# 28 filler matmuls ahead of the first TensorE operation of a fused attention and MLP kernel

## The chip, the cores and the metric

The kernel runs on one core of one Trainium2 chip. The metric is the time of one execution on the device in microseconds (us), lower is better; the median of three runs is compared.

## The reference

Four batches with eight heads, 768 positions and 64 dimensions per head. Each query may look only at six chunks of 32 keys, chosen by an upper bound; the result goes through a two-layer network with an ELU between.

```python
k_min, k_max = k_chunks.min(3), k_chunks.max(3)          # chunks of 32 keys
ub = sum(maximum(q * k_min, q * k_max), -1)              # bound per query and chunk
ub = where(causal, ub, -1e9)
top_chunks = argsort(ub)[..., -6:]
scores = where(in top_chunks and causal, (q @ k.T) / sqrt(64), -1e9)
attn_out = softmax(scores) @ v                           # (4, 8, 768, 64)
x = attn_out.transpose(0, 2, 1, 3).reshape(3072, 512)
h = x @ w_in                                             # 512 x 2048
g = where(h > 0, h, exp(minimum(h, 0)) - 1)
out = g @ w_out                                          # 2048 x 512
```

## The kernel before

The kernel first builds a list of operations (`g.op(...)`), each with its name, the engines that may run it, and the tiles that it reads and writes. Nothing is scheduled by a planner when it runs: the string `ORDER` writes the order out by hand. Each entry has three characters: the engine (P is TensorE, A ScalarE, D VectorE, G GpSimd, S the DMA queue of SyncE) and the serial number of the operation in two digits of base 64. Operations are emitted in that order, so each engine works through its own entries strictly in sequence. The string `PLACES` gives, for every tile that appears for the first time in that order, the slot of its class that it takes. The class `bank` stands for the eight PSUM banks.

```python
for j in range(0, len(order), 3):
    o = g.ops[64 * DIGITS.index(order[j + 1]) + DIGITS.index(order[j + 2])]
    for b in o.bufs:
        if b.slot is None and b.cls != "fixed":
            b.slot = DIGITS.index(next(places))
    o.emit({"P": PE, "A": ACT, "D": DVE, "G": POOL, "S": SP}[order[j]])
```

The work is cut in eight units of 384 token rows. Units 0 and 1 hold the first halves of batches 0 and 1. For them the keys and queries are loaded in pieces of 96 rows and turned by TensorE through `ident_f` (operations `kT...` and `qT...`, line 402, four f32 transposes each). VectorE reduces the keys to chunk bounds (`kmin...`, `kmax...`, line 367), and ScalarE or VectorE copy the results out of PSUM (`kt...`, `qh...`, line 320 or 322). Before the scores of the first six chunks, where no selection is needed, a mask is put into the bank by a matmul with `trineg` (`tr...`, line 676), then come the scores (`sc...`, line 684, eight matmuls), the exponentials (`ex...`, line 692) and the products with the values (`pv...`, line 746). Behind each unit's attention stand the two layers of the network: `h<unit>.<block>` (line 843, four matmuls for each of 16 column blocks of `w_in`), the exponential `e` (line 850), `m` (line 852), `g` (line 856) and the output product `o` (line 867). The network of one unit is woven between the attention of the next ones.

`w_in` is loaded by GpSimd's queue in three pieces (line 291: column blocks 0 to 3, 4 to 7, 8 to 15), `w_out` in four (line 297). Loads of `q`, `k` and `v` go into eleven slots `f` and are issued by SyncE (line 304), the first ones for `k` by ScalarE.

A filler is an operation `fill` (line 906): one matmul of a 128x128 tile of zeros with a 128x256 tile of zeros, both bf16, into a bank that nobody reads. 170 of them stand in the list of operations, and `ORDER` of the kernel before uses three, between the first transposes and masks. The tile `zeros` is set by VectorE (operation `zeros`, entry `D00`), as its sixth memset. TensorE's first entry in the kernel before is `P0M`, the key transposes `kT0p1` of batch 0.

Of the kernel before, what the change touches and what calls it, by code (L numbers as in the profile page):

```python
# [41 lines left out]
D0OD1iP1yA0LP0TS0ZPjTP1lS2hA0UA1nG16P1oGmvP1qA1sP2oGmwA1mG0-S2OD2pP18D19D13S2PP1tP1uP1vG0pA0AP1N  # L42
P1DD2qP1EA1rP25A1xA2sG0JP26A1wP1zP1AA1CG10P1ID27P1RGmxG0eG0fP1HS2RP1SD1FG0PP20D1GD28D0SGmyD1JD1K
P2aP1XA1BP1+P29G1dD1TP1YD1UP1LA1MP2wA2xP2BA2FG2HD1ZD2bD2cD1-P1OD1PP2dA2eD1QP1VA1WD21D22D12P23P2J
G2uG14A2KD24PmWAmXD2DD0oA2yGmYD2rPmSAmTPn2S2vA2ND2CG2EPm-Am+GmUGn0D2LP3lAn3DmZPmOAmPG2zDmVD3mD3n
D3pGn4Dn5PmKAmLDn1D3oGmQA2APmCAmDGmMS2ID3qGmzP38D39PmGAmHS2QGmIPnyPniDmND3rA3cAnzGnAAnjGmADmRD3a
DnkDmJPneAnfDnBA2tDnlPn6GmEA3sAn7PnaPnmAnbP3HDmFA3IGn8Dn9PnuGncAnvPnqD3tDndP3gAnnGnoGnwD3hA2GA3u
P33G3bA34A35G07P2XD2ZD2YG08A2+DnxA36DnpPnIS2VD3iGngG3jD2-S2mS3fAnrGmBG31G2WP3+A40PnPPnQD30P3JA3K
DnhP3wPnCPnDD2MD3yS2kG3vP4DD3xS32D3zD3AD3BP4jA4kD3CG3EGnsDntPnRD01S50A3FD37S2TS4ZP41A42D43S4-PnE
PnJA3dP4sA3DD2nP3QP3SA4EA4tA3TS4+S4XP4FA3RP4lG3LPnKP4aG3eA4bP48A49D2lG3US4YD2jP3NS55A4GAbeP3MD3O  # L50
G3GPnLP4MP45A4ND3kD3PG2SP4OA4PPnFA4mG4cPnSP4uAnGDnMS53G2UP4dP4eP3VG4QP44P4RAnTS7OP4SA4vD0nG4wSat
D4HP5QA5RA5SP4ID4nP4JD4fD4gD46D47P4oP3WG5TS7NP4hG5UA4iP4pD4TSnND4UP5rD3XD4qP5EA5FA5sG5uG7PD4KD4L
P4yP4xD3YS7LG5IP4VA4WP5JA5ND4zP3ZA3-P5kA5oD4rP58D4AP4BA4CD5KD5aD5LP5fA5gA5jP5xD5yPnZPoBAn-A5tA5i
S7SPopPodAoCD5lG5OD5cD59D5mSauGn+Do0G5eAoqDorA5hDoDG5nSnHG5MS5wAoeGofD5zG5APoxSnUAoyA54G56DoEPot
AouPo1GovDogDosDowAo2Go3A5GPnVAnWDo4GozG5bDoAPoJAoKS57Po9GnXAoaPo5Ao6A5HDoLDoMGobDnYDocA5dG5vA5B
PolGo7Do8AomGonP5VSaFD5XA7TD5WD5YD5ZPohAoiGojS7UPoVG5qPoFAoGA5PDooGbdPp6Po+DokPoWPoXPp7A02D5-D5+
A63A61D60P6lP6gP64ShvP6iG5pP6mA6jPp0P66S7QD7RDoHDoIA65DaGDaHA6hD62DaJA67A6nD6oP6aA6bP6uPp1P6yA6z
PoRP68A6vS51D52P6eA6fPoNA69SazAoSSavD6kP6cP6qAoOP6IPp8A6dP6pDaIDoPA6JGoTP6wA6xDoQG5DP6GDoUS7JPoY
SaKDaLDaNA6HD6KAoZG5CP6YP6MP6LA6NP6-A6ZA6+P70Pp9P6AGbjD6rA71P6EP72A73A6FPp2ScPDaMA6BScKP6CP76A6D
P74DpaP79DaOG6OP6QD6sA75A77D78P6PD6RP7aA7bD7cP7uS7MP7wA7xP7zD6SS7KS7IP7VD7WP6UA7vP6WA6VA6XSo-P7s  # L60
A7tP7ADaPP8uD8vP7mP7dD7XD7yS6TP7qA7BG7CS6tP7eD7fA7rA7nP7iDp3P7oP7kP8cA7jP85DaQA7lD7gS7hP7DA7pP7E
D8dD89G8bA8yP8pD7FD7GA8qDcQS7HA8zSaXP8iGaRPaSDaVDaWD8AP80A81D8jD8aDbkP8BA7ZA8CA8FA8DG7-D8kD8lD8w
# [36 lines left out]
AwzPw2PwiSvBGw8GwcDwdPwCAw3Dw4Dw5GwADwBPwePwIPwJAwnAwfPwuGwgDwhAwjDwkDwlPwqGwoPwOPwUAwvDw9PwKAwr
DwsDwtPwDPwEDwwDwxDwpPwFAwGSwHPwLAwMSwNPwPPwQPwRAwSSwTPwVPwWPwXAwYSwZ  # L100
"""
PLACES = """
0123450678900012310a451621724113347405105762041730373120422137035110122041374503402021750562104
11700021501212164000111000232317000261024540320151612783210206940a4115b7020263230c2d08313907563
e427013111610f2462a4157230523415317204500240181232917400132164442027121011015390433401070102214
32165110232322g012012404027056912362011513002222138302a1074000501632b12e00470a54532710053007754
3536761803040210c4d7000070514641470501540276062053123358047315654477500103751216120371201004305
1133301272500002f20031113622203117a520g015450281601270b0118e52632041024101400915211067296022454
34100764021c31306064002235167402302130631214236547406210120001573201632930716102101011702313220
34020122261030220031d151423237101000022511407221g060001258340e12213140f20009272162ab30510344272  # L110
# [845 lines left out]
```

## Time and profile before

| | |
|---|---|
| median of three runs | 286.16 us (286.0 to 286.5) |
| the profiled execution | 287.72 us, its span 286.0 us |
| TensorE matmuls busy | 267.4 us, 93% of the span |
| VectorE busy | 222.7 us, 78% |
| ScalarE busy | 208.8 us, 73% |
| GpSimd busy | 117.3 us, 41% |
| moved by DMA | 39.25 MB, mean 137 GB/s |

The span goes from the first to the last instruction of the profiled execution. Busy shares are means over stages that have different limits, and a matmul's recorded length overlaps with that of the next one, since matmuls are pipelined; the spacing of their starts is what each one costs in a row of them. PE is TensorE's matmul, PEld its weight load, DVE VectorE, ACT ScalarE, POOL GpSimd, SP SyncE; a q behind the name (SPq, ACTq, POOLq) is the sequencer of that engine, where DMAs are issued.

### The profile page before, as it was taken

To read this page: it belongs to the slowest core of one execution; us is meant where nothing else is said; L and a number is where in the kernel's file an instruction comes from. 1 tells how busy PE (TensorE), PEld (TensorE's weight loads), DVE (VectorE), ACT (ScalarE), POOL (GpSimd) and SP (SyncE) were. 2 spreads that over 40 slices of the span, in tenths; PEclk is the share of its full clock that TensorE was granted. 3 is DMA by queue.
4 is the path that set the end of the run, shared out by engine and by line. 5 is a ranking of instruction groups with operands and counts; after the bars stand their busy time and mean duration, and the time that the engine had idled before them with its cause. 6 is when DMAs were issued, how large, how long until landed. Compare 5 with 4: busy or idle time off the path is not lost.

```text
span 286.0 us, 6892 instructions
## 1 busy us (share of the span) xinstructions
PE 267.4 (93%) x2415; PEld 163.0 (57%) x2415; DVE 222.7 (78%) x674; ACT 208.8 (73%) x463; POOL 117.3 (41%) x244
## 2 busy tenths in 40 slices
PE   0898999999999899999999989899999999999995
PEld 0656665685455655476565545566556556665553
DVE  1649897689988999889799989997796989621760
ACT  0567795899599896998789569696779469792722
POOL 7484775667321275340352313501555043320510
PEclk9999999999999999999999999999999999999999
DMA  8999999979848299657984738345851420013103
GB/s 154 212 196 218 223 220 213 215 153 267 169 112 166 57 201 227 152 116 166 193 178 97 149 87 206 71 124 119 172 125 27 93 87 2 17 39 78 73 2 110
DMA packets 107107, 39.25 MB, mean 137 GB/s; under 512 B 98496, under 2 KB 102848, under 8 KB 107072
## 3 DMA queue, kind: packets, MB, share of 16 engines
q1 hardware_dynamic: 100208, 33.83, 56.6%
q0 software_dynamic: 3696, 4.19, 8.6%
q10 hardware_dynamic: 3168, 0.79, 1.7%
q8 instruction: 19, 0.31, 0.5%
q14 instruction: 16, 0.13, 0.2%
HBM read 30.41 MB, written 6.29 MB: 128 GB/s over the span
## 4 chain that ended last, share of the span: by engine, by line
PE 52%; DVE 20%; ACT 10%; DMA 5%; POOL 4%; issue 4%; SPq 3%; ACTq 0%; POOLq 0%; DVEq 0%
PE bank L867 17%; PE bank L843 14%; PE bank L774 8%; DVE gT L856 5%; PE bank L825 4%; ACT pt L789 4%; DMA xt<-on 3%; DVE kst L367 3%; DVE thr L611 3%; PE bank L543 2%; DVE m L852 2%; DMA f<-in_v_dram 2%; PE bank L592 2%; SPq L304 2%; PE bank L402 2%
## 5 line engine op out<-in xcount | busy, mean ns | idle before, releaser
L843 PE MATMUL bank<-xt,w_in_sb 128*128 128x384 bf16 x512 | 90.8, 326 | 2.2 <-DMA xt<-on 2.0
L867 PE MATMUL bank<-w_out_sb,gT 128*128 128x512 bf16 (+1 forms) x400 | 92.3, 370 | 0.0
L852 POOL TENSOR_SCALAR m<-e 128x384 f32<-128x384 f32 x90 | 46.6, 524 | 69.3 <-ACT e L850 57.8
L856 DVE SCALAR_TENSOR_TENSOR gT<-bank,m 128x384 bf16<-128x384 f32 x128 | 67.0, 549 | 7.9 <-POOL m L852 5.9
L850 ACT ACTIVATE e<-bank 128x384 f32<-128x384 f32 x128 | 59.2, 491 | 17.5 <-PE bank L843 11.5
L789 ACT ACTIVATE pt<-bank 128x384 bf16<-128x384 f32 (+1 forms) x144 | 67.3, 552 | 4.5 <-PE bank L774 4.3
L843 PEld LDWEIGHTS <-w_in_sb 128*128 128x128 bf16 x512 | 49.4, 98 | 37.0 <-issue 5.7
L867 PEld LDWEIGHTS <-gT 128*128 128x128 bf16 x400 | 37.7, 97 | 35.2 <-DVE gT L856 1.0
L774 PE MATMUL bank<-rhs,lhs 96*128 96x384 bf16 (+2 forms) x240 | 44.6, 293 | 2.2 <-DVE gT L856 0.8
L774 PEld LDWEIGHTS <-lhs 96*128 96x128 bf16 x240 | 21.7, 97 | 16.8 <-issue 3.7
L320 ACT ACTIVATE o<-bank 128x512 f32<-128x512 f32 (+1 forms) x17 | 9.8, 576 | 21.6 <-PE bank L867 19.7
L825 PEld LDWEIGHTS <-pt 128*128 128x128 bf16 x576 | 21.0, 97 | 4.9 <-DVE rcp L636 0.6
L806 POOL TENSOR_TENSOR pt<-pt,tri 128x256 bf16<-128x256 bf16 (+1 forms) x12 | 10.7, 895 | 29.4 <-ACT pt L793 16.2
L852 DVE TENSOR_SCALAR m<-e 128x384 f32<-128x384 f32 x38 | 15.4, 409 | 9.0 <-ACT e L850 8.8
L825 PE MATMUL bank<-vext,pt 128*128 128x65 bf16 x576 | 22.2, 193 | 0.1
L367 DVE TENSOR_REDUCE kst<-bank 128x12 f32<-128x384 f32 x32 | 16.6, 547 | 6.3 <-PE bank L402 3.2
L638 DVE TENSOR_TENSOR on<-bank,rcp 128x384 bf16<-128x384 f32 (+1 forms) x40 | 19.7, 502 | 1.1
L322 POOL CAST rhs<-qt 64x384 bf16<-64x384 f32 x23 | 11.5, 501 | 21.0 <-DVE qt L322 13.0
L806 DVE TENSOR_TENSOR pt<-pt,tri 128x512 bf16<-128x512 bf16 (+1 forms) x36 | 13.6, 390 | 4.8 <-ACT pt L793 3.1
L402 PE MATMUL bank<-ident_f,f 96*128 96x96 f32 x64 | 10.1, 318 | 7.5 <-POOL ident_f L254 7.5
L543 PE MATMUL bank<-ident_f,f 128*128 128x128 f32 x96 | 15.0, 277 | 0.8 <-ACT pt L789 0.7
L636 DVE RECIPROCAL rcp<-bank 128x6 f32<-128x6 f32 (+1 forms) x40 | 7.0, 182 | 10.6 <-PE bank L825 4.2
(101 smaller groups left out, 316.8 us busy)
## 6 DMA issues: line engine op xcount, KB each, us to landing
f<-in_v_dram SPq DMA_DIRECT2D x22, 256.0 KB, 4.7
out_dram<-o SPq DMA_DIRECT2D x21, 256.0 KB, 2.4
f<-in_q_dram SPq DMA_DIRECT2D x18, 256.0 KB, 4.6
f<-in_k_dram SPq DMA_DIRECT2D x18, 256.0 KB, 4.6
kc<-in_k_dram SPq DMA_DIRECT2D x8, 384.0 KB, 4.2
w_out_sb<-in_moe_w_out_dram POOLq DMA_DIRECT2D x4, 512.0 KB, 8.3
f<-in_q_dram SPq DMA_DIRECT2D x6, 192.0 KB, 5.0
w_in_sb<-in_moe_w_in_dram POOLq DMA_DIRECT2D x2, 512.0 KB, 7.5
```

Source lines behind the costliest of these rows:

```text
L367: g.op(("kmin", "kmax")[w] + tag, (DVE,), lambda e, w=w, op=op: nc.vector.tensor_reduce(out=cs(w), in_=src(), axis=AX.X, op=op), reads=[(b ...
L543: nc.tensor.transpose(ap(bk)[:, P * j:P * (j + 1)], ap(src[j])[:, P * r:P * (r + 1)], ident_f)
L638: g.op("on" + tag, (DVE,), lambda e: nc.vector.tensor_tensor(out=ap(on)[:, 0:nt].rearrange("p q h d -> p h q d"), in0=view()[:, :, :, 0:D] ...
L774: nc.tensor.matmul(ap(banks[hd])[:, o + pc:o + pc + wd], lhsT=apl(ls, G)[0:96, pr, hd, P * kb:P * (kb + 1)], rhs=ap(rs)[0:96, hd, c0 - HS ...
L789: lambda e, hd=hd, pt=pt, banks=banks, wtot=wtot: nc.scalar.activation(out=ap(pt)[:, hd, PAD:PAD + wtot], in_=ap(banks[hd])[:, 0:wtot], fu ...
L806: eng[e].tensor_tensor(out=view, in0=view, in1=tri[:, 64:64 + P].rearrange("p (a b w) -> p a b w", a=1, b=1) .to_broadcast([P, 2, len(dg), ...
L825: nc.tensor.matmul(view()[:, hd, qi, :], lhsT=ap(pt)[:, hd, P * qi + off:P * qi + off + P], rhs=ap(vx[b])[:, kb, 2 * r + hd, :], start=(kb ...
L843: nc.tensor.matmul(ap(bank)[:, 0:HS], lhsT=w_in_sb[:, kk, P * fc:P * (fc + 1)], rhs=ap(xT[i, kk]), start=(kk == 0), stop=(kk == NKK - 1))
L850: g.op(f"e{i}.{fc}", (ACT,), lambda e, eb=eb, bank=bank: nc.scalar.activation(out=ap(eb), in_=ap(bank)[:, 0:HS], func=AF.Exp), reads=[(ban ...
L852: g.op(f"m{i}.{fc}", (POOL, DVE), lambda e, eb=eb, mb=mb: eng[e].tensor_scalar(out=ap(mb), in0=ap(eb), scalar1=-1.0, scalar2=1.0, op0=AOT. ...
L856: nc.vector.scalar_tensor_tensor(out=ap(gt), in0=ap(bank)[:, 0:HS], scalar=0.0, in1=ap(mb), op0=AOT.max, op1=AOT.min),
L867: nc.tensor.matmul(ap(bank)[:, 0:d1 - d0], lhsT=ap(gts[fc])[:, P * tt:P * (tt + 1)], rhs=w_out_sb[:, fc, d0:d1], start=(fc == 0), stop=(fc ...
```

## The change

Only the two strings change. `ORDER` gets 28 more fillers directly ahead of `P0M`, so that they are the first 28 operations of TensorE; the three fillers further on stay where they are and only take the next serial numbers. `D00`, the memset of `zeros`, moves from its place behind five other VectorE memsets to the head of the list. All other entries keep their order.

`PLACES` gets a bank for each of the 28 fillers, which take the banks 0 to 7 in turn. Every later operation takes bank b + 4 where it had bank b below 4, and b - 4 where it had one of 4 to 7; slots of all other classes are the same.

```diff
 ORDER = """
-D0cG0gG0jD0hG0lG06S0XS0BD09A0uD0kS0xG0dD03A0sG04A0rA0tA0WG0qA0VS0vD00S0YG0bS0zS0wS0yG0aP0MA0QA0R
-D05P1pP1jPjRGcZD0iD0NS2iD0mP0DP1aD0CD0ED0FG0GP11A15G17PjSS2gS2fD1cS0+P1kD1eD1fG1gA0HA0IP1hD1bP0K
...
+D00D0cG0gG0jD0hG0lG06S0XS0BD09A0uD0kS0xG0dD03A0sG04A0rA0tA0WG0qA0VS0vS0YG0bS0zS0wS0yG0aPjRPjSPjT
+PjUPjVPjWPjXPjYPjZPj-Pj+Pk0Pk1Pk2Pk3Pk4Pk5Pk6Pk7Pk8Pk9PkaPkbPkcPkdPkePkfPkgP0MA0QA0RD05P1pP1jPkh
+GcZD0iD0NS2iD0mP0DP1aD0CD0ED0FG0GP11A15G17PkiS2gS2fD1cS0+P1kD1eD1fG1gA0HA0IP1hD1bP0KD0OD1iP1yA0L
...
 PLACES = """
-0123450678900012310a451621724113347405105762041730373120422137035110122041374503402021750562104
...
+01234506789012345670123456701234567012340056710a01122132411734300114536200133437756402253307515
...
 """
```

More of the change, by code (lines that the diff above doesn't have):

```diff
@@ L45 @@
[L45 to L62, printed above, removed]
@@ new lines @@
+P25A1xA2sG0JP26A1wP1zP1AA1CG10P1ID27P1RGmxG0eG0fP1HS2RP1SD1FG0PP20D1GD28D0SGmyD1JD1KP2aP1XA1BP1+
+P29G1dD1TP1YD1UP1LA1MP2wA2xP2BA2FG2HD1ZD2bD2cD1-P1OD1PP2dA2eD1QP1VA1WD21D22D12P23P2JG2uG14A2KD24
+PmWAmXD2DD0oA2yGmYD2rPmSAmTPn2S2vA2ND2CG2EPm-Am+GmUGn0D2LP3lAn3DmZPmOAmPG2zDmVD3mD3nD3pGn4Dn5PmK
+AmLDn1D3oGmQA2APmCAmDGmMS2ID3qGmzP38D39PmGAmHS2QGmIPnyPniDmND3rA3cAnzGnAAnjGmADmRD3aDnkDmJPneAnf
+DnBA2tDnlPn6GmEA3sAn7PnaPnmAnbP3HDmFA3IGn8Dn9PnuGncAnvPnqD3tDndP3gAnnGnoGnwD3hA2GA3uP33G3bA34A35
+G07P2XD2ZD2YG08A2+DnxA36DnpPnIS2VD3iGngG3jD2-S2mS3fAnrGmBG31G2WP3+A40PnPPnQD30P3JA3KDnhP3wPnCPnD
@@ new lines @@
+D2MD3yS2kG3vP4DD3xS32D3zD3AD3BP4jA4kD3CG3EGnsDntPnRD01S50A3FD37S2TS4ZP41A42D43S4-PnEPnJA3dP4sA3D
+D2nP3QP3SA4EA4tA3TS4+S4XP4FA3RP4lG3LPnKP4aG3eA4bP48A49D2lG3US4YD2jP3NS55A4GAbeP3MD3OG3GPnLP4MP45
+A4ND3kD3PG2SP4OA4PPnFA4mG4cPnSP4uAnGDnMS53G2UP4dP4eP3VG4QP44P4RAnTS7OP4SA4vD0nG4wSatD4HP5QA5RA5S
+P4ID4nP4JD4fD4gD46D47P4oP3WG5TS7NP4hG5UA4iP4pD4TSnND4UP5rD3XD4qP5EA5FA5sG5uG7PD4KD4LP4yP4xD3YS7L
+G5IP4VA4WP5JA5ND4zP3ZA3-P5kA5oD4rP58D4AP4BA4CD5KD5aD5LP5fA5gA5jP5xD5yPnZPoBAn-A5tA5iS7SPopPodAoC
+D5lG5OD5cD59D5mSauGn+Do0G5eAoqDorA5hDoDG5nSnHG5MS5wAoeGofD5zG5APoxSnUAoyA54G56DoEPotAouPo1GovDog
@@ new lines @@
+DosDowAo2Go3A5GPnVAnWDo4GozG5bDoAPoJAoKS57Po9GnXAoaPo5Ao6A5HDoLDoMGobDnYDocA5dG5vA5BPolGo7Do8Aom
+GonP5VSaFD5XA7TD5WD5YD5ZPohAoiGojS7UPoVG5qPoFAoGA5PDooGbdPp6Po+DokPoWPoXPp7A02D5-D5+A63A61D60P6l
+P6gP64ShvP6iG5pP6mA6jPp0P66S7QD7RDoHDoIA65DaGDaHA6hD62DaJA67A6nD6oP6aA6bP6uPp1P6yA6zPoRP68A6vS51
+D52P6eA6fPoNA69SazAoSSavD6kP6cP6qAoOP6IPp8A6dP6pDaIDoPA6JGoTP6wA6xDoQG5DP6GDoUS7JPoYSaKDaLDaNA6H
+D6KAoZG5CP6YP6MP6LA6NP6-A6ZA6+P70Pp9P6AGbjD6rA71P6EP72A73A6FPp2ScPDaMA6BScKP6CP76A6DP74DpaP79DaO
+G6OP6QD6sA75A77D78P6PD6RP7aA7bD7cP7uS7MP7wA7xP7zD6SS7KS7IP7VD7WP6UA7vP6WA6VA6XSo-P7sA7tP7ADaPP8u
@@ new lines @@
+D8vP7mP7dD7XD7yS6TP7qA7BG7CS6tP7eD7fA7rA7nP7iDp3P7oP7kP8cA7jP85DaQA7lD7gS7hP7DA7pP7ED8dD89G8bA8y
+P8pD7FD7GA8qDcQS7HA8zSaXP8iGaRPaSDaVDaWD8AP80A81D8jD8aDbkP8BA7ZA8CA8FA8DG7-D8kD8lD8wA82G84A8ED7+
+PpEApFD86D8xPpMApNPpgD87ShuGbgGpGDpHD8rGpODpPA8mPpcApdGpeDpfPpIPpwApJGpKAphA8eD8fApxG7YA8gPpoG88
+DpLPpAApBGpiDpjA8sGpCDpDPpQSaBApRGpyG83DpzP8GD8ID8KAppScMGpSDpTPpsAptGpuSayDpvAaCPpkPq0SnOPq4ScT
+GpqAplScRAq1AcSD8HGpmAq5PpYDpnA8tD8JApZGq6DprGp-PpUS8hAcUScJAaAPq8PqoPqpAq9D8LD8MApVDq7PqcPqdGpW
+DpXA8NP8TP8+Dp+SaDP8VPqqSawAaEScOA90A8WGqaDaYSpbG8OP8RDqbAaTDaUA8UP93A94Dq2A8SP91DaZDq3P96P97A98
@@ new lines @@
+GbhSaxSbiA92ScNDa+P8XA8YPqeP8ZA8-Sb0P9tA9uP9rA9sPqrD8QPafAagD95D99P9aD8PP9pA9qP9fP9bD8oPahD9cD9d
+A9gG9vP9lA9mP9nA9oGcVP9xP9wA9yDqsPqfG8nDqgP9jPalAaiP9hA9iA9kPbrDa-P9LP9TA9UP9RA9SDbsP9XP9WA9YG9z
+P9BP9AP9NA9OA9MShpDb1D9CD9ZD9DS9EPd2PadP9FA9GPakSqhP9PA9QP9JA9KDajPabAacP9HShzGcYD9VDb2PbBA9IPa3
+Aa4Pa5Aa6Db4AaeP9-DbCP9+AamPbmDa0SflDa1Pa7Pa9AaaPqiDanAa8DbuS9ePapDbFGbESa2DbnPaoDaqAboAd3PbwAbx
+DarDb3PqjPqkPqlDb6SasDbyDbvDb5AbqAqmDbtGb7PdhSqtPb8Db9DbbPqyGbAAqzDbcPqOAqPAcWGqQDfmDfnAbaSp4AbD
+DqADqBDqRPraArbPquGrcPqCAqDAbpDrdPbGDbHAdiDbJAqvPdcAd4AddPriPr2GqEArjDqFDqwPd7DbIDbKGrkAr3Gr4Drl
@@ new lines @@
+DbLPqWAqXDbMPr6Ar7Gr8DqxDr9PqGAd8DqYDqZPreAqHPqSScLDc+AbOAqTPrqDbNPqKGbQDr5GqIDqJAbPArrGrsDrtAqL
+SblSbfPc3Ac4ScXGqUPrmDqMDqNDqVSfaArnGbzPq-Aq+Dr0PbTAbUPrADr1PbWArfPbXAhIGrgSc-DfpAbYPc5Ac6Dc7PrB
+PcBPbRAbSDfoPcmSf9SqnDg0PcASfqAd0PcxAcyPrCDdaPruAcCAdePc8PcjPc9PcvDd9PcnGcDGroDrhPrvPrwAckAcwSfj
+Sd1DbVDbZPb+AcaDcbPcdPchDczPcEPb-AcoShtDrpDd5AciDc0SfbPccDc1Sc2DcePcFDcfAdbScgPrDDcGDcpAdjGclGhw
+DcHScIPdmArESrFDdnPcqPcrDcsDctPrGScuPrxAryAf+PrHPrIPrJDdpAdfArKPsgAshDdoDdqDdrDdsPscAsdPrQAduDfr
+DfsPrYArRDdtPdBGdlDseArZDsfDsiDsjAdCGd6PdzDfuPe5PsoAe6Gr-Dr+AspDsqAdAGrSSfcDrTPrMArNPdHAdIPs4As5
@@ new lines @@
+GrODrPPrUDfWArVGrWGhASfIPsAPe9SfeAsBDsrPdFAdGDrXPs8As9AeaDsCPe3Ae4PskSrzDs6PdJDsDPswDs7DdvPsIPe7
+AslDsmPs0DsnAsxPsMDsaPdXGsyDszAsJSfdDsKAdKAs1Gs2DsLPdOAhCDs3PdPAdQGfZPsEAdYPdLPdDAdEAdMShrDsbPsN
+GdgAsFAe8PdxSg1DftAdyDfwSffPdZPssPsSGfkAd-DdNDdRPdTDfvGfxDdwPedAstDsuPfyDfzAfADsvPdSDdUDdVSdWDeb
+Pe1Ae2DfJAfBAfCDfKPsTPd+PecAe0SrLAeePexDefPezGfYPeCPeDAeEAfVPsODeFPenAeADfMPevAewGsGDsHSfDPehAey
+PegAeoDeiDejDeBSekGdkPghGhBPetAeuPsPAsQPeXPelAemPf1DfLPeZPf0DgiPg2PepAf2PsUAeqPerPeGDg3Gg6Dg4AeY
+AesAe-PeNAeOPeLPeVAeMDe+PePPeHPeRDeISp5DeJShsPeTSeKPg7Dg8Gf3AeQPsVDsWSsXAeUAeSPgcPf4AeWPf5DfEDf6
@@ new lines @@
+AgdDf7PsYPsZAglPhKAhLGhOPs-DfFDfHAgkDggPs+Sf8AgeDfODfGDfNGfPPtGPtuDg9AhHPfQAt0AtHGtIDfTAfUDtJPtC
+AtDDtEAfRDfSDtFAtvGtwDtxAgjGgfPtiPtaAtbGtcPgmDgoAhMPt6At7GfgGt8PteAtfGtgDgqDtdDgnDgpShDDgrPtmAtn
+GtoDt9PtKAtLGtMDgsPt2At3PtSAtjAguDtpDtNGtkDtlPtWSsRPtqPtyGt4SfXDgtPt-PtODt5AgvDthPu8AtrDtsDttDg5
+Sf-PgxAtXPgzGtYDtZAtTAtzPu9GtADtBSfhPhUPhPAtPGtUDtVShqAhEAgyPuaAgwPhgDgbDtQAt+DtRPhbAgAGgBSt1AhQ
+AhVAhcGhYAhRPgRPhdDu0AhePgCPgDAgEDgFPu2Pu3DhXGgaPgQAgSDhfPh3DhWPhhAhiGhFPgZShxShGAg-Ph2Ah4GfiPhZ
+Ah-Pg+Ah0Ah+GhyPu4PgNDgTAgOShJDu1PgGPgHDgIDhjPubDh1AucGh5DgJPhlPhkPh6SgKPh7Dh8Dh9ShaPgLAgMDgPDhm
@@ new lines @@
+75005073116165203312010007011533301232104002f20035113262203113a120g015050285201270b4118e1623204
+102010140495121106329242205434104760025c7130602004267552704230617023125067214344665012000113724
+523697475210610145130271322030020122225430620031d111027233501004026111403221g020041258740e52613
+104f20009232122ab301107402324206467152030441173621638553677472060413523016121060250211131117200
+106002c2044526141022757235611d50020141210a30017200b5e4722121612032a2100851f33074166151921437225
+1710121012325314075090502322720315076123242061767030185313012620122100131014523001g722410536201
@@ L118 @@
+01004223100a0701d5220112036c1e047256f0121130422120730701352322283024216407500321422674632794210
+3740356112501226421110761300124220b14305052060a1021d310f41112210113554062272e0144607362025c0711
+0g17240220335617001413080061202730634561711635203445023471212702451302030227010129150004124600a
+16011305230041015612b12322142c01e02311f01708d2012
 """
```

70 lines of the change are left out of this document (15 added, 55 removed).

## The prediction

> **What bounds the kernel now.** I read the page first (span, busy shares, the forty slices), then the chain of waits for the first 30 us, then the timeline of TensorE alone there, and last those of VectorE, ScalarE and GpSimd.
>
> ```profile
> span 286.0 us, 6892 instructions
> ...
> PE   0898999999999899999999989899999999999995
> ...
> PEclk9999999999999999999999999999999999999999
> ```
>
> TensorE is busy in nearly every slice but the first, which is empty: nothing runs there for 7.46 us. The granted clock reads full throughout, so if the array is slow anywhere, that row does not say so; durations must.
>
> ```profile
> 7.46 0.90 PE L402 MATMUL bank<-ident_f,f 96*128 96x96 f32 x4 [7.46 <-POOL ident_f L254]
> 9.68 0.42 PE L906 MATMUL bank<-zeros 128*128 128x256 bf16 x1
> 9.89 2.13 PE L402 MATMUL bank<-ident_f,f 96*128 96x96 f32 x12
> 11.81 0.42 PE L906 MATMUL bank<-zeros 128*128 128x256 bf16 x1
> 12.03 0.63 PE L676 MATMUL bank<-trineg,ident_b 128*128 128x512 bf16 x1
> 12.46 1.58 PE L402 MATMUL bank<-ident_f,f 96*128 96x96 f32 x8
> 15.81 0.61 PE L684 MATMUL bank<-xt,kt 64*128 64x64 bf16 x8
> 21.52 0.40 PE L684 MATMUL bank<-xt,kt 64*128 64x64 bf16 x8
> 25.70 0.83 PE L661 MATMUL bank<-ident_b,on 128*128 128x128 bf16 x8 [0.67 <-ACT xt L320]
> 26.37 0.50 PE L402 MATMUL bank<-ident_f,f 96*128 96x96 f32 x4
> ```
>
> In each row stand the start, the length (both us), the engine, line, operation and tiles, and the idle time before it with what ended it. The same four transposes take 0.90 us at 7.46 and 0.50 at 26.37; the same eight score matmuls 0.61 at 15.81 and 0.40 at 21.52. So the array runs at about half speed from its first instruction to a little after 21 us, and at full speed afterwards, whatever the clock row says. Those are the 14 us that the change can touch. In them TensorE sets the end only for a part:
>
> ```profile
> 7.46 0.92 PE bank L402 x4
> ...
> 8.45 1.28 ACT L320
> ...
> 10.27 0.56 DVE kst L367
> ...
> 13.77 0.48 DVE kst L367
> ...
> 14.29 0.58 PE bank L676
> ...
> 20.36 0.94 PE bank L746 x15
> ...
> 21.96 0.60 ACT pt L692
> ```
>
> The chain goes through TensorE for the first four transposes, through ScalarE and VectorE from 8.45 to 14.25, and through TensorE again from 14.29 to 21.9. Only the first and the last of these gain from a faster array.
>
> **The change part by part.** *The fillers' own cost.* They need only `zeros`, whose memset moves to the head of VectorE's queue.
>
> ```profile
> 0.96 0.38 DVE L247 MEMSET econst<- 32x384 bf16 x1 [0.96 <-PEq L940]
> 2.60 0.17 DVE L247 MEMSET zeros<- 128x128 uint32 x1
> 9.26 0.15 PEld L906 LDWEIGHTS <-zeros 128*128 128x128 bf16 x1 [0.28 <-issue]
> ```
>
> VectorE starts at 0.96; 0.17 us of memset, about 0.05 us of hand-over and 0.15 us of weight load put the first filler at about 1.33. A slow filler is recorded at 0.42 us, but the matmul behind it starts 0.21 (9.68 to 9.89) and 0.22 us (11.81 to 12.03) later: matmuls overlap, and the price is about 0.213. 28 of them take 5.97 us and free the array at 7.30. The first transposes wait for `ident_f` until 7.46, so the fillers lie wholly in an idle stretch, with 0.16 us to spare; once the clock rises they go faster still. At 0.22 each they would end at 7.49 and cost 0.03. If the cover were gone, each filler would cost its 0.21 in full. The five VectorE memsets that `zeros` is moved past start 0.17 us later. `ident_f`'s own memset stands just ahead of the 2.60 of this row, and the first transposes are released by GpSimd's work on it only at 7.46, so that costs nothing. No queue of loads is touched. All later PSUM banks are renumbered by one fixed swap of 0-3 with 4-7, so who waits for whose bank stays the same: nothing.
>
> *What the fillers buy.* The trace shows when the clock rises in the kernel before (just after 21 us, at the end of a dense run of score and value matmuls) but not how much work it takes, so this is bounded from both sides: no release before 7.46 (nothing gained), or a full release (below). I take the release, since almost 6 us of back-to-back 128-row matmuls are denser than the mix of transposes, short matmuls and waits that did not suffice between 7.46 and 21. [...]
>
> With the array fast from 7.46 on:
> First transposes: 0.90 becomes 0.50, so the table load at 8.45, the copy and all of VectorE's run from 10.27 to 14.25 come 0.40 earlier. That run itself is not shortened.
>
> ```profile
> 13.70 1.01 DVE L367 TENSOR_REDUCE kst<-bank 128x12 f32<-128x384 f32 x2
> 15.70 0.49 ACT L320 ACTIVATE xt<-bank 128x384 bf16<-128x384 f32 x1 [1.14 <-PE bank L402]
> 16.46 0.60 ACT L692 ACTIVATE pt<-bank 128x512 bf16<-128x512 f32 x1 [0.27 <-PE bank L684]
> 17.54 1.08 ACT L692 ACTIVATE pt<-bank 128x512 bf16<-128x512 f32 x2 [0.48 <-PE bank L684]
> 20.40 0.60 ACT L692 ACTIVATE pt<-bank 128x512 bf16<-128x512 f32 x1 [0.78 <-PE bank L684]
> 21.27 1.78 ACT L692 ACTIVATE pt<-bank 128x512 bf16<-128x512 f32 x3
> ```
>
> The reduce pair ends at 14.71, or 14.31 after; it frees the bank for `qT0p1`, whose four transposes then take 0.50: done at about 14.85, and ScalarE's copy `qh0p1` starts at 14.9 instead of 15.70. That is 0.8 in all. From there ScalarE becomes the bound: between 15.70 and the exponential at 21.96 it waits for TensorE 0.27 + 0.48 + 0.78 = 1.53 us and works the rest. With scores in half the time these waits go, and nothing shortens the exponentials. So at 22 us the kernel is at most 0.8 + 1.53 = 2.3 us ahead.
>
> *What is late next.* Weights. The first layer's last eight column blocks of `w_in` come in one GpSimd load, here with its issue, its time to landing, and the matmuls that use it:
>
> ```profile
> 19.82 0.79 POOL L291 DMA_DIRECT2D w_in_sb<-in_moe_w_in_dram  x1
> DMA to landing us min/median/max: 12.4/12.4/12.4
> 32.50 4.71 PE L843 MATMUL bank<-xt,w_in_sb 128*128 128x384 bf16 x28
> ```
>
> It lands at 32.2. Of the 28 matmuls the first four (`h0.1`) use the earlier load; the fifth (`h0.15`) starts at 32.50 + 4 x 0.168 = 33.17, less than 1 us after the landing. TensorE 2.3 us ahead would want it at 30.9. How far the load moves I bound by 0.4 (its queue on GpSimd moves with the VectorE run) and 2.3 (it moves with TensorE). I take 0.4, since the transfers around it queue rather than idle: 12.4 us for 1 MB. It then lands at 31.8, and 33.17 - 31.8 = 1.4 us is what remains, because TensorE runs without a gap from there through all 28. Behind it I find no load that comes closer to its user than this, so I carry 1.4 us to the end: the work there waits for work, not for a fixed time.
>
> Sum: span 286.0 - 1.4 = 284.6; the profiled execution's own 287.72 becomes 286.3, and the median of the three runs, 286.16, becomes 284.8. A difference under 0.2% (0.6 us) is about what a measurement of this kernel cannot tell from none.
>
> **The rivals.** *The load is no limit* and the whole 2.3 us survives: 283.9. For it: loads ahead of it are issued earlier as well, so the engines may have time left. Against: it took 12.4 us in a full queue.
>
> *The release fails or is lost again.* [...] The trace speaks against the loss: around 25.70 a stretch of transposes with a wait of 0.67 leaves the clock up. [...] Then at most the first 0.40 us remains: 285.8 to 286.2, no difference.
>
> *The fillers outlast their cover*: slower. If each cost its recorded 0.42 us, because every one waits for the one before or for its weights, 28 take 11.8 us, from 1.33 to 13.1, and the first transposes start 5.6 us late; 2.3 come back through the fast array and some 3.3 remain: 289.5. The turning point is sharp: (7.46 - 1.33) / 28 = 0.219 us each, and up to about 0.30 the gain still pays for it (28 x 0.08 = 2.2). Against it stand the two spacings of 0.21 and 0.22, though each is of one filler among other matmuls and none of fillers in a row on cycling banks.
>
> **How the numbers follow.** Forecast (released, load-limited) 0.50; load no limit 0.18; no release or lost again 0.18; fillers outlast their cover 0.10; the rest, 0.04, for a reshuffle of loads and queues that gives most of the gain back. Predicted 284.8. The range reaches from the full 2.3 us with a little over (283.5) to the no-difference case (286.5, the slowest of the runs shown); it leaves out the slower rival. Faster by over 0.2%: 0.50 + 0.18 and a little of the third, 0.70. Same: 0.18. Slower: 0.12.
>
> **What would show it.** Right: 28 fillers between about 1.3 and 7.3 on TensorE, spaced 0.21 and then 0.11; the first four transposes still at 7.46 but in 0.50 us; eight score matmuls near 15 in 0.40; ScalarE without waits between 15 and 20; the exponential of 21.96 near 19.7; TensorE waiting before `h0.15` for a load. Wrong: transposes still at 0.90; the first of them later than 7.5, released by nothing but TensorE itself; a VectorE run that does not come forward; or a front that is 2 us ahead at 22 us while the end is not.

## The result, and the profile after

| | changed kernel | kernel before, beside it |
|---|---|---|
| median of 11 runs each | 285.39 us (285.04 to 285.93) | 286.68 us (286.0 to 288.84) |
| the profiled execution | 285.42 us, span 283.7 us | 287.72 us, span 286.0 us |

The ratio is 0.9945, with a 95% interval of 0.9924 to 0.9966: the change makes the kernel faster by about 0.55%, or 1.6 us. (The means of the eleven runs, 285.42 and 287.00, lie 1.6 us apart, the medians 1.3. The profiled execution of the kernel before is 1.0 us above its median, so two profiles compared show a larger gain than the runs do.) Forecast were 284.8 us in a range of 283.5 to 286.5, and faster with a chance of 0.70. So the size came out as forecast. The runs below show that the reason did not.

First the page of the changed kernel, with the rows that stood in the prediction for the kernel before, and the row of q8, a queue of instructions that becomes important further on:

```profile
span 283.7 us, 6948 instructions
...
PE   8788999999999899999999999899999999999995
...
PEclk9799999999999999999999999999999999999999
...
q8 instruction: 19, 0.31, 0.5%
```

The empty first slice is filled. The clock row now has a dip in its second slice. The timeline of TensorE (start, length, engine, line, operation and tiles, idle time before with its releaser) shows the first 36 us:

```profile
1.14 6.10 PE L907 MATMUL bank<-zeros 128*128 128x256 bf16 x28 [1.14 <-DVE zeros L248]
7.48 0.55 PE L403 MATMUL bank<-ident_f,f 96*128 96x96 f32 x4 [0.24 <-POOL ident_f L255]
...
10.44 1.54 PE L403 MATMUL bank<-ident_f,f 96*128 96x96 f32 x8 [0.50 <-DMA f<-in_k_dram]
...
15.09 0.40 PE L685 MATMUL bank<-xt,kt 64*128 64x64 bf16 x8
...
25.33 1.96 PE L844 MATMUL bank<-xt,w_in_sb 128*128 128x384 bf16 x11 [0.64 <-DMA w_in_sb<-in_moe_w_in_dram]
...
31.52 0.47 PE L403 MATMUL bank<-ident_f,f 96*128 96x96 f32 x3 [0.46 <-DMA f<-in_k_dram]
31.82 4.71 PE L844 MATMUL bank<-xt,w_in_sb 128*128 128x384 bf16 x28
```

The fillers, each 0.21 us behind the other, end at 7.24, the first transposes start at 7.48, released by `ident_f` as before, and need 0.55 us in place of 0.90. The first score matmuls need 0.40 in place of 0.61. But the eight transposes at 10.44 take 1.54: they are slow again. The windows view of the changed kernel says why (window; its length; busy time and count of PE, PEld, DVE, ACT and POOL; granted clock; DMA share; GB/s):

```profile
7.15:10.60 3.45, 1.84 (x13) 1.23 (x13) 1.38 (x4) 2.30 (x3) 1.92 (x5) 0.98 1.34 213
10.60:14.05 3.45, 3.38 (x19) 2.81 (x19) 3.42 (x9) 1.51 (x4) 1.49 (x4) 0.52 1.36 209
14.05:21.50 7.45, 6.47 (x99) 4.23 (x99) 4.71 (x15) 6.05 (x12) 5.73 (x10) 1.00 1.29 197
```

The clock that the fillers raised was lost at about 10.5, after a stretch in which TensorE was busy for 1.84 of 3.45 us, and was back at about 13.9 (shorter windows read 1.00 for 10.35 to 10.45, 0.50 for 10.50 to 10.60 and for 13.70 to 13.85, and 1.00 for 13.90 to 14.00). While it was lost VectorE was busy for 3.42 of 3.45 us and set the pace, so the loss cost next to nothing there. ScalarE's timeline shows how the front came forward:

```profile
15.02 0.49 ACT L321 ACTIVATE xt<-bank 128x384 bf16<-128x384 f32 x1 [0.59 <-PE bank L403]
15.53 1.74 ACT L693 ACTIVATE pt<-bank 128x512 bf16<-128x512 f32 x3
...
19.87 1.08 ACT L693 ACTIVATE pt<-bank 128x512 bf16<-128x512 f32 x2 [0.19 <-PE bank L685]
```

The copy `qh0p1` starts at 15.02 in place of 15.70, and of the 1.53 us of waits behind it 0.19 is left. The exponential that started at 21.96 belongs to the pair at 19.87. The front is 2.1 us ahead at 22 us. That is one execution; f3_oldbanks below, with the same 28 full fillers, was 0.25 us ahead there.

From there two waits in TensorE's timeline above take it back: 0.64 for a piece of `w_in` at 25.33 and 0.46 for a load of keys at 31.52. The chain of waits names the second one:

```profile
15.02 0.31 SPq L305
...
15.38 16.09 DMA f<-in_k_dram
...
31.52 0.47 PE bank L403 x3
```

The key load took 16.09 us to land, where the same load took 9.1 in the kernel before. TensorE's row behind it is 0.7 us ahead (31.82 against 32.50); on ScalarE 1.0 us of the lead is left from 36 to 87 us. Then it grows again, to 3.0 us at 172, and is 2.28 at the end. The fast array cannot do that: it has been equally fast in both kernels since 22 us (eight score matmuls take 0.40 at 21.52 in the kernel before; a matmul of the first layer takes 326 ns on average in both pages, one of the second 370). So the end gains about what was forecast, but most of it arises behind 87 us, from something that the prediction had not thought of.

### The profile page after: what moved, and what is told of

It reads as the page before. It is cut to its first block, busy times and chain, and to the rows that moved or that the text cites. A ratio compares the mean times of both kernels' runs of the same rounds, so it can differ in the third digit from the quotient of the medians.

```text
span 283.7 us, 6948 instructions
## 1 busy us (share of the span) xinstructions
PE 270.5 (95%) x2443; PEld 164.8 (58%) x2443; DVE 222.1 (78%) x674; ACT 208.5 (73%) x463; POOL 117.5 (41%) x244
## 4 chain that ended last, share of the span: by engine, by line
PE 64%; DVE 14%; DMA 11%; ACT 4%; POOL 3%; issue 3%; SPq 0%; POOLq 0%; ACTq 0%; DVEq 0%
PE bank L868 21%; PE bank L844 20%; PE bank L775 10%; DMA f<-in_k_dram 6%; PE bank L826 5%; DVE gT L857 4%; DMA xt<-on 3%; PE bank L544 3%; PE bank L593 2%; DMA f<-in_v_dram 2%; DVE m L853 2%; DVE thr L612 1%; DVE kst L368 1%; ACT pt L790 1%; PE bank L403 1%
## 5 line engine op out<-in xcount | busy, mean ns | idle before, releaser
L639 DVE TENSOR_TENSOR on<-bank,rcp 128x384 bf16<-128x384 f32 (+1 forms) x40 | 19.7, 502 | 1.1
L323 POOL CAST rhs<-qt 64x384 bf16<-64x384 f32 x23 | 11.5, 502 | 21.0 <-DVE qt L323 13.0
L794 ACT ACTIVATE pt<-bank 128x512 bf16<-128x512 f32 x24 | 14.4, 612 | 0.2 <-PE bank L775 0.2
```

Of the source, the lines that this page charges most:

```text
L639: g.op("on" + tag, (DVE,), lambda e: nc.vector.tensor_tensor(out=ap(on)[:, 0:nt].rearrange("p q h d -> p h q d"), in0=view()[:, :, :, 0:D] ...
```

## The experiments

Every kernel below computes all of the reference, and each was timed in five rounds (10 to 12 runs, of e3_48 five). Ratios are to the kernel before on the same chip, where its medians were 286.59, 287.26 and 287.45 us in the three groups.

**Is it the clock?** The theory of the prediction: the raised clock moves the front, and what the loads leave of that reaches the end. The rivals: the gain comes from the new bank numbers or the early memset, or the added instructions themselves move something later. *e1_narrow* keeps 28 fillers, banks and memset, and takes the work out of the fillers:

```diff
-        fills.append(g.op("fill", (PE,), lambda e, bank=bank: nc.tensor.matmul(
-            ap(bank)[:, 0:256], lhsT=zeros[:, 0:P], rhs=zeros, start=True, stop=True),
+        fills.append(g.op("fill", (PE,), lambda e, bank=bank, w=32 if i < 28 else 256: nc.tensor.matmul(
+            ap(bank)[:, 0:w], lhsT=zeros[:, 0:P], rhs=zeros[:, 0:w], start=True, stop=True),
```

> The 28 fillers stay in their place, with the early memset and the renumbered banks, but each streams 32 columns instead of 256. Theory (the gain is the clock's): 28 short matmuls are done by about 3 us and do not raise the clock, so the first four transposes again take 0.90 us, the eight score matmuls near 15.8 again 0.61, and the time is that of the kernel before, within 0.3%. Rival (the banks, the memset or a TensorE queue that is already running bring the gain): the time stays near the changed kernel's, 0.5% under the kernel before, with slow transposes at 7.5 us.

TensorE's timeline of this kernel:

```profile
1.14 0.93 PE L907 MATMUL bank<-zeros 128*128 128x32 bf16 x28 [1.14 <-DVE zeros L248]
7.48 0.90 PE L403 MATMUL bank<-ident_f,f 96*128 96x96 f32 x4 [5.41 <-POOL ident_f L255]
...
15.82 0.61 PE L685 MATMUL bank<-xt,kt 64*128 64x64 bf16 x8
...
21.65 0.40 PE L685 MATMUL bank<-xt,kt 64*128 64x64 bf16 x8
```

Transposes in 0.90, scores in 0.61 until 21 us: the clock did not rise, and the front stands where it stood before. Yet the kernel takes 285.47 us, ratio 0.9956 (0.9936 to 0.9976). With the change it was 0.9945. The theory of the clock falls here, as a theory of the time.

Part of this 0.44% may be chance. Of the 27 executions of the kernel before that were timed beside it, five have a mean granted clock of 0.993 or 0.994 and took 287.7 us on average, the other 22 took 286.3; none of the ten of e1_narrow is below 0.998. Against those 22 it is ahead by 0.24%, give or take 0.14.

*e2_half* puts 14 full fillers ahead, *e3_48* puts 48:

```diff
-...Pj-Pj+Pk0Pk1Pk2Pk3Pk4Pk5Pk6Pk7Pk8Pk9PkaPkbPkcPkdPkePkfPkgP0MA0QA0R...
+...Pj-Pj+Pk0Pk1Pk2P0MA0QA0R...
```

> 14 fillers of 256 columns instead of 28. Theory (the clock needs a whole stretch of dense work, which ended near 7.2 us in the changed kernel): 14 end near 4.2 us, the clock stays down, first transposes at 0.90 us, time as before within 0.3%. Rival (the clock needs only some 3 us of work from a cold start, and 28 fillers are more than needed): the clock rises by 7.46 us, first transposes at about 0.55, time as with 28, some 0.5% under the kernel before.

```diff
-...PkcPkdPkePkfPkgP0MA0QA0R...
+...PkcPkdPkePkfPkgPkhPkiPkjPkkPklPkmPknPkoPkpPkqPkrPksPktPkuPkvPkwPkxPkyPkzPkAP0MA0QA0R...
```

> 48 fillers, 20 more than the cover holds. The clock rises near 7.2 us as with 28, and the 20 more cost about 0.11 us each: they end near 9.4 us and the first transposes start about 1.9 us late. Theory (loads, not TensorE, limit what is left at 32 us): part of the delay disappears in the waits for the load of w_in at 25 us and of keys at 31 us, and the kernel is 0.2% to 0.4% faster than before still. Rival (all of the front's lead reaches the end): 1.9 us of delay take away all of the gain and a little more, no faster than before.

e2_half: 285.79 us, 0.9985 (0.9962 to 1.0009), no difference that shows. Its profile, in TensorE's timeline, had the first transposes still slow, as the theory said, but the clock up by the time of the scores:

```profile
7.48 0.90 PE L403 MATMUL bank<-ident_f,f 96*128 96x96 f32 x4 [3.17 <-POOL ident_f L255]
...
15.44 0.40 PE L685 MATMUL bank<-xt,kt 64*128 64x64 bf16 x8
...
26.20 4.45 PE L844 MATMUL bank<-xt,w_in_sb 128*128 128x384 bf16 x16 [1.50 <-DMA w_in_sb<-in_moe_w_in_dram]
```

It was 2.05 us ahead at 19.5 us, then waited 1.50 for `w_in`, lost the clock once more (16 matmuls of the first layer in 4.45 us, where the kernel before needs 2.77 at 26.70), and was 1.2 behind at 35 us. So a front that is 2 us ahead can be gone 15 us later.

e3_48: 289.16 us, 1.0086 (1.0062 to 1.0110). That is slower than both of its expectations. Its fillers outlast the cover, which the prediction had as a rival for 28 of them:

```profile
1.14 8.02 PE L908 MATMUL bank<-zeros 128*128 128x256 bf16 x48 [1.14 <-DVE zeros L249]
8.99 0.50 PE L404 MATMUL bank<-ident_f,f 96*128 96x96 f32 x4
```

The first transposes start 1.5 us late. This run can't be read for the count alone.

*e4_keepwarm* adds 12 more full fillers where the clock was lost, eight behind the first transposes and four behind the next ones, so that the stretch ahead of 10.5 is full:

```diff
-...P0MA0QA0RD05P1pP1jPkh
-GcZD0iD0NS2iD0mP0DP1aD0C...
+...P0MPkhPkiPkjPkkPklPkmPknPkoA0QA0RD05P1pP1jPkp
+GcZD0iD0NS2iD0mP0DPkqPkrPksPktP1aD0C...
```

> As the changed kernel, with 8 more fillers behind the first transposes and 4 behind the next four, in stretches where TensorE waits, so that the clock does not fall back at 10.6 us. If it holds, the eight transposes at 10.44 take 0.88 us instead of 1.54. Theory (from 9.9 to 14.4 us VectorE's reduces set the pace, so the lost clock cost nothing): time as the changed kernel within 0.2%. Rival (the 3.4 us at half clock cost something): about 0.3% to 0.5% faster than the changed kernel.

It held the clock, as TensorE's timeline shows (eight transposes in 0.88, before 1.54), and it is slower: 287.58 us, 1.0031 (1.0011 to 1.0052). Neither expectation had that.

```profile
7.87 1.04 PE L907 MATMUL bank<-zeros 128*128 128x256 bf16 x8
...
10.59 0.88 PE L403 MATMUL bank<-ident_f,f 96*128 96x96 f32 x8 [0.21 <-DMA f<-in_k_dram]
...
136.38 0.49 PE L844 MATMUL bank<-xt,w_in_sb 128*128 128x384 bf16 x2 [0.51 <-DMA xt<-on]
137.31 2.51 PE L844 MATMUL bank<-xt,w_in_sb 128*128 128x384 bf16 x13 [0.44 <-DMA xt<-on]
```

The loss of the clock had indeed cost nothing: at the copy `qh0p1` it is 0.69 us ahead, the changed kernel 0.68. It was 1.2 us ahead of the kernel before until 135 us, and level with it at 142, by the two waits of the last rows.

**Banks, memset, or a load?** *f1_banks* is the kernel before with the banks swapped, *f2_memset* the kernel before with the memset of `zeros` first, *f3_oldbanks* the changed kernel with the old banks. *e6_ec_late* is the changed kernel with two loads of constants moved behind the next query load, to keep them from the key load that cost 0.46 us.

```diff
-0123450678900012310a451621724113...
+0123450678940056710a011221324117...
```

> The kernel before with nothing changed but the banks, 0-3 and 4-7 swapped. Theory A (narrow fillers gained 0.4% because the new bank numbers are better): some 0.4% faster than before. Theory B (what a kernel gains at the end is decided by which transposes and loads come late after 90 us, and any small shift of the start can throw that): the banks alone shift nothing, within 0.2% of before. Theory C (the early memset or the fillers' instructions did it): within 0.2% too.

```diff
-D0cG0gG0jD0hG0lG06S0XS0BD09A0uD0kS0xG0dD03A0sG04A0rA0tA0WG0qA0VS0vD00S0YG0b...
+D00D0cG0gG0jD0hG0lG06S0XS0BD09A0uD0kS0xG0dD03A0sG04A0rA0tA0WG0qA0VS0vS0YG0b...
```

> The kernel before with nothing changed but the memset of zeros, moved to the head of VectorE's queue. The start should shift by no more than 0.02 us. Theory A (banks): no change. Theory B (small shifts decide): anything within 0.3% of before, with a lead or loss that arises only after 90 us. Theory C (early memset): some 0.4% faster.

```diff
-01234506789012345670123456701234567012340056710a011221324117343...
+01234506789012345670123456701234567012300012310a451621724113347...
```

> The changed kernel with its 28 full fillers and early memset, but every later operation on the bank that it has in the kernel before. Theory A (banks): the gain falls to 0.1% or less. Theory of the clock: the front is 2.1 us ahead at 22 us, as in the changed kernel, and the time 0.3% to 0.6% under before.

```diff
-PmTPn2S2vA2ND2C...GmMS2ID3qGmzP38D39PmGAmHS2QGmI
+PmTPn2A2ND2C...GmMD3qGmzP38D39PmGAmHS2QS2vS2IGmI
```

> The changed kernel with the two broadcast copies lhs<-econst of batch 0 issued behind the query load that follows them on SyncE's queue. In the changed kernel the first of them held that queue from 18.5 to 25.9 us and the key load issued just before it took 16 us to land, where it took 9 us in the kernel before. Theory (the copies' small packets crowd out the loads): the key load lands by 27 us, the wait of 0.46 us at 31.5 goes, the lead at 42 us is 1.4 us or more instead of 1.0, and the time is up to 0.2% under the changed kernel's. Rival (the weight loads crowd it out, or the landing differs from run to run): the key load still lands after 30 us.

f1_banks 287.18 us, 0.9990 (0.9968 to 1.0011); f2_memset 287.50 us, 1.0001 (0.9978 to 1.0023): neither has an effect that shows. f3_oldbanks 285.88 us, 0.9952 (0.9929 to 0.9974): the 28 fillers gain without the new banks. They did so without the front as well. In the profile of f3_oldbanks the clock fell a little after 14 us (four transposes take 0.55 at 12.79 and 0.90 at 14.41), where TensorE is needed, the scores took 0.61 until 19.4, and the front was 0.25 us ahead at 22 us and not the 2.1 that had been expected. e6_ec_late 286.23 us, 0.9969 (0.9948 to 0.9990), no better than the change. In its profile the key load lands after 11.5 us, at 27.5, and the wait for it is gone, but TensorE waits further on for the constants that were put back:

```profile
31.41 0.49 PE L403 MATMUL bank<-ident_f,f 96*128 96x96 f32 x4
31.74 4.72 PE L844 MATMUL bank<-xt,w_in_sb 128*128 128x384 bf16 x28
36.97 0.38 PE L721 MATMUL bank<-rhs,lhs 96*128 96x128 bf16 x3 [0.51 <-DMA lhs<-econst]
```

Its front was not 2 us ahead in this execution, so what the wait would cost a front that is stays open.

**Is it the number of instructions?** So far 28 fillers, full or narrow, gave 0.995 to 0.996, and 40 gave 1.003. The theory now is that the count on TensorE decides, whatever the fillers do. The rival is that e4_keepwarm was slow by the places of its 12 extra fillers. Narrow ones of 8 columns, all ahead of the first transposes, tell them apart: *g_40n* 40, *g_64n* 64, *g_128n* 128; *g_28f12n* has 12 narrow ones and then 28 full ones.

```diff
-        fills.append(g.op("fill", (PE,), lambda e, bank=bank: nc.tensor.matmul(
-            ap(bank)[:, 0:256], lhsT=zeros[:, 0:P], rhs=zeros, start=True, stop=True),
+        fills.append(g.op("fill", (PE,), lambda e, bank=bank, w=8 if i < 40 else 256: nc.tensor.matmul(
+            ap(bank)[:, 0:w], lhsT=zeros[:, 0:P], rhs=zeros[:, 0:w], start=True, stop=True),
```

> 40 fillers of 8 columns ahead of the first transposes, no full ones: done by about 2.5 us, clock not raised. Theory N (the end depends on how many instructions stand ahead on TensorE, not on the clock: 28 gain 0.45%, 40 lost 0.3%): 0.1% to 0.5% slower than before. Theory E (any early work on TensorE brings the gain, and the 12 more fillers lost it by where they stood): 0.45% faster, as 28 narrow ones.

> 64 fillers of 8 columns. Theory N: some value between 0.5% faster and 0.5% slower that is not that of 28, with a front as in the kernel before up to 85 us. Theory E: 0.45% faster.

> 128 fillers of 8 columns, with their weight loads 256 instructions, as many as one 16 KB fetch of TensorE's instructions holds by its packets in the trace; done by about 6 us, inside the cover. Theory N in its narrow form (the place of the instruction fetches decides, and 256 more put them back where they were): within 0.2% of before. Theory E: 0.45% faster. A value apart from both: the number matters, but not by that period.

> 12 fillers of 8 columns, then the 28 full ones of the changed kernel: front and clock as in the changed kernel (the full ones start some 0.4 us later and end by 7.6), 40 more matmuls in all. Theory N: as the kernel with 12 more fillers behind the first transposes, no faster than before. Theory E: 0.5% faster than before, as the changed kernel.

In the third column, slow stands for eight score matmuls in 0.60 or 0.61 us and four transposes in 0.85 to 0.90, fast for 0.40 and 0.49 to 0.55.

| kernel | fillers | array in its profile, 7.5 to 21 us | us | ratio to before |
|---|---|---|---|---|
| changed kernel | 28 full | fast but for 10.5 to 13.9 | 285.39 | 0.9945 (0.9924 to 0.9966) |
| f3_oldbanks | 28 full | fast to 14, then slow | 285.88 | 0.9952 (0.9929 to 0.9974) |
| e1_narrow | 28 narrow | slow | 285.47 | 0.9956 (0.9936 to 0.9976) |
| e4_keepwarm | 40 full | fast | 287.58 | 1.0031 (1.0011 to 1.0052) |
| g_28f12n | 12 narrow, 28 full | fast to 10.7, then slow | 288.22 | 1.0032 (1.0012 to 1.0052) |
| g_40n | 40 narrow | slow, fast by 14.3 | 288.54 | 1.0037 (1.0011 to 1.0063) |
| g_64n | 64 narrow | slow, fast from 12.4 | 289.72 | 1.0070 (1.0045 to 1.0094) |
| g_128n | 128 narrow | slow, fast from 18.9 | 288.36 | 1.0041 (1.0018 to 1.0064) |

The groups of runs were made on different chips, so only the ratios of different groups can be compared; e1_narrow and e4_keepwarm ran on one chip, 2.1 us apart. Three kernels with 28 fillers agree within 0.0011, and three with 40 within 0.0006; e6_ec_late, with 28 and two loads moved, is at 0.9969. Within each group the array was fast, half fast or slow; the width, the places and the banks differ too. Between the groups lie 0.8%. With executions of a granted clock of 0.997 or more alone, e1_narrow is at 0.998 and e4_keepwarm at 1.004, still 0.6% apart. That the number separates 28 from 40, and not the clock, is shown. It is no price per instruction: 14 did nothing that shows, 28 gain, 40 lose, and 128 lose less than 64. The narrow form of theory N, that 256 more instructions bring the time back to within 0.2% of before, fails with 1.0041.

**Where the two groups part.** The start of the same ScalarE instruction against that in the kernel before, in us (negative is ahead), from the profiled executions:

| in the kernel before at | 22 | 82 | 134.7 | 142.3 | 172 | end |
|---|---|---|---|---|---|---|
| changed kernel (28) | -2.09 | -0.96 | -2.12 | -2.10 | -3.02 | -2.28 |
| e1_narrow (28) | +0.13 | -0.09 | -0.96 | -1.00 | -1.92 | -1.38 |
| f3_oldbanks (28) | -0.25 | -0.48 | -1.09 | -1.40 | -2.41 | -1.69 |
| e4_keepwarm (40) | -1.75 | -1.18 | -1.20 | -0.01 | 0.00 | +0.71 |
| g_40n (40) | -2.03 | -0.21 | -0.37 | +0.72 | +0.78 | +0.69 |
| g_28f12n (40) | -0.23 | -0.29 | -0.49 | +0.53 | +0.56 | +0.66 |
| f1_banks (3, as before) | -0.16 | -0.23 | -1.00 | -0.91 | -1.15 | -0.63 |

The lead at 22 us says nothing of the end: g_40n was 2 us ahead there and ends behind, e1_narrow was not and ends ahead. All with 40 lose 1.0 to 1.2 us between 134.7 and 142.3, and none with 28. All with 28 gain 0.9 to 1.0 between 142.3 and 172, and none with 40. The 28s also gain 0.6 to 1.2 between 82 and 134.7, the 40s 0.0 to 0.2; but f1_banks, which is no faster than the kernel before, gains 0.8 there too. So this part need not come from the fillers: it also tells that the profiled execution of the kernel before was a long one.

The first of these places is a row of three DMA transposes. SyncE's timelines of the kernel before, the changed kernel, e4_keepwarm, g_40n and g_28f12n, in this order:

```profile
132.19 3.81 SPq L649 DMA_TRANSPOSE xt<-on  x3
```

```profile
129.76 3.86 SPq L650 DMA_TRANSPOSE xt<-on  x3
```

```profile
130.67 5.04 SPq L650 DMA_TRANSPOSE xt<-on  x3
```

```profile
131.50 5.03 SPq L650 DMA_TRANSPOSE xt<-on  x3
```

```profile
131.39 4.85 SPq L650 DMA_TRANSPOSE xt<-on  x3
```

In e1_narrow it is 3.86 as well. With 40 fillers they hold SyncE's queue 1.0 to 1.2 us longer, and TensorE waits for them, as in the two waits of e4_keepwarm above. The time to landing parts the kernels better than the time in the queue. Of the same three transposes, in the changed kernel and then in g_64n, each counted from its own issue:

```profile
DMA to landing us min/median/max: 3.1/4.3/4.5
```

```profile
DMA to landing us min/median/max: 4.4/5.4/6.5
```

From the first issue to the last landing they take 5.3 to 5.8 us in nine kernels (3, 14, 28 or 128 fillers) and 6.8 to 7.0 in five (40, 48 or 64). In these five TensorE waits 0.8 to 1.4 us for them, and all five lose 1.0 to 1.2 us between 134.7 and 142.3; in the nine the wait is at most 0.4. The queues that moved something between 130 and 137 us (packets, MB, share) tell what else ran there. First e1_narrow, then g_40n:

```profile
q1 hardware_dynamic: 2724, 1.55, 100.5%
q14 instruction: 1, 0.01, 0.4%
```

```profile
q1 hardware_dynamic: 2450, 1.19, 104.1%
q14 instruction: 1, 0.01, 1.6%
q8 instruction: 1, 0.02, 1.1%
```

q8 has 19 packets of 16 KB in the whole kernel before. The profile names no engine for it. I take it for the queue that fetches TensorE's instructions: 4830 matmuls and weight loads over 19 packets are 254 for each; the tenth packet starts behind 1255 matmuls in the kernel before (at 141.9 us) and behind 1247 in the changed one (at 138.3), though 28 more stand ahead there; and g_128n, with 128 matmuls more, has one packet more. The packet that starts at 141.9 us in the kernel before starts at 137.9 to 139.2 with 28 fillers, when the three transposes have landed, and at 133.4 to 134.9 with 40, while they are under way. It falls within their time in e3_48 and g_64n as well (135.6 and 137.0), where the row in SyncE's queue is 3.86 and 3.87 but TensorE waits for the landing all the same. In g_128n it is at 141.2, about where it was before, and there are 20 packets in all. So the number of instructions moves the fetches, though not evenly: 48 and 64 do not bring this one further forward than 40. That the fetch is what holds the transposes up fits all fourteen traces, but no run moved a fetch and nothing else: it is argued, not shown.

The second place is the output. The waits between 148 and 168 us in the kernel before, and then in the changed kernel (engine, tile, line, what it waited for; us in all, times, longest):

```profile
ACT o L320 <- PE bank L867: 3.0, 1, 3.0
...
ACT o L320 <- DMA out_dram<-o: 1.8, 1, 1.8
...
PE bank L843 <- DMA xt<-on: 1.0, 1, 1.0
```

```profile
ACT o L321 <- PE bank L868: 4.2, 2, 3.0
```

Before, a copy into an output tile waits 1.8 us until an earlier store has landed, and TensorE 1.0 for a DMA transpose. In the changed kernel, e1_narrow and f3_oldbanks both are gone; with 40 fillers both are there (1.9 to 2.0, and 1.0 to 1.1), and in f1_banks too (1.5 and 0.8).

What stays open: how much of the gain between 82 and 134.7 us the fillers bring, why the order of stores and transposes comes out better near 158 us with 28, and where g_128n loses. Its profiled execution (287.41 us) lies 1.0 us under its median, and has neither the late transposes nor the fetch there. At the front it waited 1.77 us for a key load at 12.5, where the others waited at most 1.04.

## Why the prediction was right in size and wrong in its reason

**The fillers' cost: right.** They started at 1.14, not 1.33 (the memset ended at 1.09, so the hand-over took the 0.05 of the sum, but the first matmul's record begins with that of its weight load), ended at 7.24, not 7.30, and the first transposes were not moved (7.48 for 7.46). The spacing stayed at 0.21; the 0.11 that had been forecast for the last ones did not come, since the clock rose only at their end. The rival that they outlast their cover was e3_48's, with 48, not this kernel's.

**The release: right, with half of a rival beside it.** That almost 6 us of fillers would be enough was an estimate: behind the 14 of e2_half, which ended at 4.31, the first transposes still took 0.90. Here the clock rose as the fillers ended, at about 7.1 (the 28th is recorded at 0.36 us, those ahead of it at 0.42), and was lost again once, which stood in the rival "the release fails or is lost again". In the changed kernel's profile it was lost where VectorE binds, was down from about 10.5 to 13.9, and came back after a stretch of 18 matmuls of which 16 were f32 transposes against an identity. In those of f3_oldbanks and g_28f12n it stayed down until about 21 us and the front was 0.25 and 0.23 us ahead at 22, as that rival had it; yet f3_oldbanks gained about as much as the changed kernel, and not the "no difference" of the rival.

**The front: right for the profiled execution.** 0.50 forecast and 0.55 measured for the first transposes; `qh0p1` 14.9 and 15.02; the exponential near 19.7 and 19.87; 2.3 us ahead at 22 us and 2.1.

**"What is late next. Weights": the wrong load.** I took the third piece of `w_in` at `h0.15`; TensorE did not wait there. It waited 0.64 us for the second piece at 25.33 and 0.46 for a key load at 31.52, so 0.7 to 1.0 us was left and not 1.4. The bound that failed was "I find no load that comes closer", with a margin worked out for one load alone: the key load landed after 16.09 us in place of 9.1.

**"I carry 1.4 us to the end: the work there waits for work, not for a fixed time": wrong.** This is the step that made the sum, and it failed: the number was met by luck, with 1.6 us that came about in another way. Behind 87 us the lead changes at transfers, up and down by 0.5 to 1.2 us at a time. Neither e1_narrow's gain without a front nor e4_keepwarm's loss with one can come from it. That the raised clock adds something is not excluded: at 28 fillers the full ones stand 0.0011 better than the narrow ones, with about 0.003 of uncertainty on this difference, so it is worth 0.3 us, give or take 0.8; at 40 the full ones stand 0.0005 better. 2.1 us it is not.

**The rivals.** The case "a reshuffle of loads and queues that gives most of the gain back" had 0.04. A reshuffle is what happened, with the other sign, and I had given a gain from it no chance at all. An honest sum would have held two terms: a front worth 0 to 1.4 us, and an unknown of about 1.5 us to either side for everything behind it that moves, since kernels with 28 and 40 such fillers lie 2 to 3 us apart.

## What to carry to other kernels

A lead at the front is worth what is left of it at the next transfers (here 1.0 of 2.1 us behind two loads), so follow the same instruction's start in both traces along the whole span before the front is called the cause. When instructions are added, also run them emptied of their work in the same number, and run another number: here 28 idle fillers gained about as much as 28 working ones (0.44% against 0.55% and 0.48%), and 40 lost. Compare the executions' granted clocks as well before a difference of half a percent is given a cause. A gain of half a percent that comes in this way is bound to this exact list of instructions, and may go with the next edit.

## What the runs showed of the hardware that was not expected

- In the changed kernel the granted clock read 1.00 at 10.35 to 10.45 us and 0.50 at 10.50 to 10.60, at the end of 3.45 us (7.15 to 10.60) in which TensorE was busy for 1.84; it read 1.00 again at 13.90 to 14.00, at the end of 3.45 us (10.60 to 14.05) in which it was busy for 3.38. In the kernel before, 14 us of mixed transposes and short matmuls (busy for 13.27 of 14.35 us by the record, 7.15 to 21.50) had not raised it until 21. In f2_memset, whose TensorE has the same list of instructions, eight score matmuls took 0.40 at 16.68 already, where they took 0.61 at 16.89 in the kernel before: the moment differs between executions.
- The same three DMA transposes took 5.3 to 5.8 us from first issue to last landing in nine kernels and 6.8 to 7.0 in five, and a packet of 16 KB on q8 started while they were under way in these five only. That it is the cause is not shown.
- 40 matmuls of 8 columns took 1.23 us at the start, at the head of an idle stretch of 6.3, and the kernel with them was 0.37% longer at the end (g_40n, 1.0011 to 1.0063).
